# Hash attention with a SwiGLU layer: one pair's load moved between two groups of hash-bit DMAs, one head's hash moved by a slot

## The chip, the cores and the metric

The kernel runs on one core of one Trainium2 chip. The metric is device time in microseconds (us) of one execution; lower is better.

## The reference

Four batches, eight heads, 768 tokens, head width 64. Each query and key is hashed to six sign bits, and a query attends only to keys of the same bucket. The result goes through an RMS norm and a SwiGLU layer.

```python
q_bits = (einsum('bhsd,dk->bhsk', q, proj) > 0)      # proj: 64 x 6
k_bits = (einsum('bhsd,dk->bhsk', k, proj) > 0)
mask = q_bucket[:, :, :, None] == k_bucket[:, :, None, :]
scores = where(mask, q @ k.T / sqrt(64), -1e9)
attn = softmax(scores)                                # with 1e-9 in the sum
x = (attn @ v), heads side by side                    # 3072 x 512
xn = x / sqrt(mean(x * x) + 1e-6) * rms_g
out = (silu(xn @ w_gate) * (xn @ w_val)) @ w_out      # 512 -> 1536 -> 512
```

## The kernel before

**The work.** A unit `w` is half a batch of queries (384), so there are eight units, two to a batch. A *pair* (b, hp) is two neighbouring heads of batch b; (1, 3) is batch 1's last pair, heads 6 and 7. A *slot* is one step of 256 keys for one head and unit: `scores` (L338) makes two matmuls into PSUM, `probs` (L349) takes the exponential on ScalarE (ACT), and some slots later `av` (L357) multiplies with v. There are 192 slots. Slots 0 to 47 are batch 0's two units, in the order of `TURNS`; from slot 48 on units 2 to 7 follow, 24 slots each. Unit 2's pairs (1, 0), (1, 1), (1, 2), (1, 3) begin at slots 48, 54, 60 and 66.

**How masking works.** The tile `QK` holds a pair's k and q in fp16, 64 rows of data and twelve rows of hash bits below them. The bits are scaled so that unequal buckets push the score far down. So slot 48 can be computed only when rows of data *and* rows of bits of its pair are there.

**A pair's way.** The rows of k and q are loaded by SyncE (SP): `load_rows` (L107) as one DMA of 384 KB, or, for pairs (1, 2) and (1, 3) and all of batches 2 and 3, `load_blocks` (L115), four DMAs of 96 KB in short rows. Transposes on TensorE (PE) with a copy on VectorE (DVE) (`keep_pair`, L169 and L177), or, for the block-loaded pairs, on DVE alone (`turn_dve`, L193) give `T0`, the fp32 transposed form. Casts on GpSimd (POOL) and ACT bring it to `QK`. For the hash, small fp32 matmuls on PE (`hash_bank`, L209) fill a PSUM bank, and one DVE instruction (`signs`, L216) makes the bits. These then move to their twelve rows: as DVE copies and one SP DMA per head for heads 2 and 3 (`hash_head`, L247 and L249), or as eight SP DMAs per pair in batch 1 (`hash_pair`, L267, for pairs (1, 0) and (1, 1); `hash_lone`, L284, for (1, 2) and (1, 3)).

**Order.** It is written out by hand. `plan[s]` lists what is emitted at slot s, and `at(s, f, ...)` adds to it; ranks order the entries of a slot, equal ranks keep the order in which they were added. Each step of the last loop emits `scores(s + 1)`, the entries of rank below 3, `probs(s + 1)`, and then the rest. Each engine works its own instructions in that order, so one that waits holds those behind it. SP issues all loads of q, k and v, the bits DMAs and the stores; the weights are loaded by POOL (L520, L526). At most eight of SP's DMAs are under way at once: the ninth waits for the first of them to land, since they use eight semaphores in turn.

**Buffers.** The raw rows of q, k and v share ten buffers (`lpool`), taken in order of emission. Hash, transposes, gate, value and projection share three PSUM banks (`gps`). Scores have two PSUM buffers of their own.

**Around the change.** Head 2 of batch 0 is the first of pair (0, 1). Its k and q are transposed at slots 1 and 2, those of head 3 at slots 4 and 5. Its bits are needed from slot 12 on. Batch 1's pairs (1, 0) and (1, 1) are hashed at slots 32 and 41, each with eight bits DMAs on SP. The k, q and v of (1, 3) are loaded at slots 42, 44 and 47; its k is transposed by DVE at slots 52 to 55, its q at 56 to 59. From slot 48 on unit 0's SwiGLU layer runs between the scores: `gate` (L445, then a tanh on ACT, L447, and `a` on DVE, L457) and `value` (L455, L458).

Of the kernel before, what the change touches and what calls it, by code (L numbers as in the profile page):

```python
# [43 lines left out]
def kernel(  # L44
# [528 lines left out]
    def at(s, f, *a, rank=3):  # L573
        plan[s].append((rank, len(plan[s]), lambda: f(*a)))
# [23 lines left out]
            at(s + 1, casts, 0, hp, i)  # L598
        at(sv, v_prep, 0, hp)

    for h, s in ((2, 3), (3, 7)):
        at(s, hash_one, h)
        for t in range(3):
            at(s + 1 + t, lambda h=h, t=t: moves[h]((nc.vector,), t), rank=5)
# [26 lines left out]
    def in_row(loads, s, hash_slot=None):  # L631
        return loads, range(s, s + 8), (s + 4, s + 8, s + 9), hash_slot

    work = {
        (1, 2): ((21, 23, 30), (36, 37, 40, 40, 48, 49, 50, 51), (42, 52, 46), 53),
        (1, 3): in_row((42, 44, 47), 52, 61),
        (2, 0): in_row((51, 56, 59), 61), (2, 1): in_row((64, 67, 70), 71, 80),
        (2, 2): in_row((73, 76, 79), 81), (2, 3): in_row((82, 85, 88), 91, 100),
        (3, 0): in_row((94, 98, 102), 106), (3, 1): in_row((104, 108, 112), 116, 125),
# [118 lines left out]
```

## Time and profile before

| | |
|---|---|
| device time, median of 3 runs | 337.61 us (337.46 to 338.91) |
| profiled execution: its own time | 339.3 us |
| profiled execution: span, first to last instruction | 337.5 us |
| granted TensorE clock | 0.999 |
| PE, DVE, ACT, POOL busy | 326.8, 236.4, 210.0, 155.3 us |
| SP's DMA queue (q1), POOL's (q0) | 26.09 MB, 4.72 MB |

All times inside the execution are us from the span's start. A timeline line gives start, duration, engine, line, operation, output and inputs, count, and in brackets the idle time ahead of it with what ended it. Neighbouring instructions of one kind are merged ("x4"). "SPq" is SP's issuing of a DMA, not the transfer. In a table by stretches each engine has its busy time and, in brackets, its instructions, then come the granted clock, the mean busy share of the 16 DMA engines, and GB/s. In the list of waits the numbers are us in total, times, and the longest.

### The profile page before, as it was taken

The page shows a single profiled execution, that of the slowest core. Times are in us where ns is not written, and L with a number is a line of the kernel's source. Part 1 is how long each engine was busy: PE and PEld are TensorE (multiplying, and loading weights), DVE is VectorE, ACT ScalarE, POOL GpSimd, SP SyncE. Part 2 cuts the span into 40 slices and gives each one's busy share as a digit, 9 for nine tenths or more (in the row PEclk, how much of TensorE's full clock was granted, in tenths as well). Part 3 has the DMA queues.
Part 4 walks back from the last instruction along what each step waited for, and adds up shares of the span by engine and source line. Part 5 has one row for each costly group of instructions (what it writes and reads, how often), then busy time and mean ns, then how long its engine had stood idle before and what let it go on. Part 6 is the DMA issues. An engine that isn't in the chain of part 4 may idle for free.

```text
span 337.5 us, 7796 instructions
## 1 busy us (share of the span) xinstructions
PE 326.8 (97%) x2993; PEld 201.0 (60%) x2993; DVE 236.4 (70%) x526; ACT 210.0 (62%) x328; POOL 155.3 (46%) x230
## 2 busy tenths in 40 slices
PE   8999989889999999999999999999999999999995
PEld 7566656455566565566555666566556665655653
DVE  4769798688758896668768897557546663883860
ACT  3789987656666575757666676567667675332321
POOL 4878789836465576245736475613111311110000
PEclk9999999999999999999999999999999999999999
DMA  7999999464376064508243261100010001001002
GB/s 238 330 223 260 169 169 187 75 124 100 79 186 118 15 111 119 104 20 168 69 105 84 44 116 64 35 16 0 33 62 2 3 0 64 33 0 64 32 0 93
DMA packets 80244, 31.36 MB, mean 93 GB/s; under 512 B 65240, under 2 KB 77264, under 8 KB 80208
## 3 DMA queue, kind: packets, MB, share of 16 engines
q1 hardware_dynamic: 76272, 26.09, 31.7%
q0 software_dynamic: 3712, 4.72, 8.8%
q8 instruction: 23, 0.38, 0.5%
q14 instruction: 13, 0.11, 0.1%
q10 hardware_dynamic: 224, 0.07, 0.1%
HBM read 28.32 MB, written 6.29 MB: 103 GB/s over the span
## 4 chain that ended last, share of the span: by engine, by line
PE 85%; DVE 6%; SPq 3%; DMA 2%; ACT 2%; issue 1%; DVEq 0%; ACTq 0%
PE y_ps L469 18%; PE v_ps L455 17%; PE s_ps L343 15%; PE g_ps L445 12%; PE o_ps L365 9%; PE s_ps L445 5%; PE d_ps L209 4%; SPq L267 2%; PE t_ps L169 1%; PE x_ps L430 1%; PE z_ps L336 1%; DMA kL<-in_k_dram 1%; DVE otmp L380 1%; DVE xn L423 1%; ACT psb L353 1%
## 5 line engine op out<-in xcount | busy, mean ns | idle before, releaser
L353 ACT ACTIVATE psb<-s_ps 128x768 f16<-128x768 f32 x192 | 150.8, 808 | 28.1 <-PE s_ps L343 26.9
L343 PE MATMUL s_ps<-QK 76*128 76x384 f16 x384 | 93.5, 325 | 1.3 <-ACT psb L353 0.5
L455 PE MATMUL v_ps<-xnT,wv 128*128 128x384 f16 x384 | 78.1, 326 | 0.1
L469 PE MATMUL y_ps<-wo,ht 128*128 128x512 f16 x276 | 69.2, 379 | 0.3 <-ACT ysb L476 0.3
L389 POOL TENSOR_TENSOR x<-otmp,rcp 128x384 f32<-128x384 f32 x31 | 25.7, 830 | 93.0 <-DVE rcp L385 92.7
L365 PEld LDWEIGHTS <-psb 128*128 128x128 f16 x1152 | 51.6, 97 | 25.5 <-issue 7.5
L447 ACT ACTIVATE t<-g_ps 128x384 f32<-128x384 f32 x72 | 35.3, 490 | 43.6 <-PE g_ps L445 43.4
L458 DVE SCALAR_TENSOR_TENSOR ht<-a,v_ps 128x384 f16<-128x384 f32 x96 | 53.2, 554 | 10.7 <-PE v_ps L455 1.5
L457 DVE SCALAR_TENSOR_TENSOR a<-t,g_ps 128x384 f32<-128x384 f32 x72 | 39.5, 548 | 28.5 <-ACT t L447 28.3
L445 PE MATMUL g_ps<-xnT,wg 128*128 128x384 f16 x288 | 58.6, 325 | 0.7 <-DVE a L457 0.5
L365 PE MATMUL o_ps<-vl,psb 128*128 128x65 f16 x1152 | 56.8, 194 | 0.6 <-DVE otmp L380 0.5
L455 PEld LDWEIGHTS <-wv 128*128 128x128 f16 x384 | 36.4, 97 | 23.9 <-issue 0.5
L445 PEld LDWEIGHTS <-wg 128*128 128x128 f16 x384 | 36.0, 97 | 24.4 <-issue 1.1
L343 PEld LDWEIGHTS <-QK 76*128 76x128 f16 x384 | 31.6, 98 | 16.1 <-issue 3.7
L469 PEld LDWEIGHTS <-ht 128*128 128x128 f16 x276 | 25.9, 97 | 24.0 <-issue 0.6
L476 ACT COPY ysb<-y_ps 128x512 f32<-128x512 f32 x23 | 13.5, 585 | 25.5 <-PE y_ps L469 22.8
L431 DVE TENSOR_TENSOR xnT<-x_ps,gcol 128x512 f16<-128x512 f16 x24 | 16.3, 685 | 15.1 <-PE x_ps L430 15.1
L401 POOL TENSOR_TENSOR sq<-x 128x384 f32<-128x384 f32 x31 | 25.6, 826 | 2.4
L380 DVE TENSOR_TENSOR otmp<-o_ps,cvb 128x390 f32<-128x390 f32 x32 | 17.8, 558 | 8.8 <-PE o_ps L365 8.7
L447 ACT ACTIVATE t<-s_ps 128x384 f32<-128x384 f32 x24 | 11.8, 491 | 18.4 <-PE s_ps L445 17.6
L201 POOL CAST QK<-kT 64x768 f16<-64x768 f32 x20 | 16.8, 838 | 12.4 <-DVE kT L193 6.5
L193 DVE STREAM_TRANSPOSE kT<-kL 128x192 f32<-128x192 f32 x40 | 19.8, 517 | 2.7 <-DMA kL<-in_k_dram 2.7
(80 smaller groups left out, 325.7 us busy)
## 6 DMA issues: line engine op xcount, KB each, us to landing
vL<-in_v_dram SPq DMA_DIRECT2D x16, 384.0 KB
out_dram<-ysb SPq DMA_DIRECT2D x23, 256.0 KB
kL<-in_k_dram SPq DMA_DIRECT2D x40, 96.0 KB
qL<-in_q_dram SPq DMA_DIRECT2D x40, 96.0 KB
kL<-in_k_dram SPq DMA_DIRECT2D x5, 384.0 KB
qL<-in_q_dram SPq DMA_DIRECT2D x5, 384.0 KB
wg<-in_moe_w_gate_dram POOLq DMA_DIRECT2D x2, 768.0 KB, 7.2
wv<-in_moe_w_val_dram POOLq DMA_DIRECT2D x2, 768.0 KB, 8.5
```

The costliest lines, as they stand in the source:

```text
L343: nc.tensor.matmul(ps[:, j, 0:HALF], k_cols(w // 2, h, 2 * p + j), q_cols(w, h), start=True, stop=True,)
L353: nc.scalar.activation(psb[w, h][:, p], sps.pop(g)[:, :, 0:HALF], AF.Exp, scale=ESCALE,)
L365: nc.tensor.matmul(o[:, c, hh, 0:65], psb[w, h][:, jt // 2, jt % 2, 128 * c : 128 * c + 128], vls[b % 2][:, h, v_chunk(b, h, jt), 0:65], s ...
L380: nc.vector.tensor_add(tmp[:, :, :, 0:65], o[:, :, :, 0:65], cvb[b % 2][:, 2 * hp : 2 * hp + 2, 0:65].unsqueeze(1).to_broadcast([128, 3, 2 ...
L389: eng.tensor_mul(xd.rearrange("p c (h d) -> p c h d", h=2), tmp[:, :, :, 0:64], r.to_broadcast([128, 3, 2, 64]),)
L401: nc.gpsimd.tensor_mul(sq, xd, xd)
L445: nc.tensor.matmul(g, wg[:, kt, fs], xnT[w][:, kt], start=(kt == 0), stop=(kt == 3))
L447: nc.scalar.activation(t, g, AF.Tanh, scale=0.5)
L455: nc.tensor.matmul(vv, wv[:, kt, fs], xnT[w][:, kt], start=(kt == 0), stop=(kt == 3))
L457: nc.vector.scalar_tensor_tensor(out=a, in0=t, scalar=1.0, in1=g, op0=ALU.add, op1=ALU.mult)
L458: nc.vector.scalar_tensor_tensor(out=ht[w][:, ft], in0=a, scalar=0.5, in1=vv, op0=ALU.mult, op1=ALU.mult)
L469: nc.tensor.matmul(y, ht[w][:, ft, c * 128 : (c + 1) * 128], wo[:, ft, :], start=(ft == 0), stop=(ft == NF - 1),)
```

## The change

Two numbers of the written-out order. Head 2 of batch 0 is hashed at slot 4 instead of 3; its three DVE copies of bits, always one to three slots after it, move along. The k of pair (1, 3) is loaded at slot 38 instead of 42, and its q at 43 instead of 44; v stays at 47.

```diff
-    for h, s in ((2, 3), (3, 7)):
+    for h, s in ((2, 4), (3, 7)):
         at(s, hash_one, h)
         for t in range(3):
             at(s + 1 + t, lambda h=h, t=t: moves[h]((nc.vector,), t), rank=5)
...
     work = {
         (1, 2): ((21, 23, 30), (36, 37, 40, 40, 48, 49, 50, 51), (42, 52, 46), 53),
-        (1, 3): in_row((42, 44, 47), 52, 61),
+        (1, 3): in_row((38, 43, 47), 52, 61),
```

What it moves in each engine's order: on PE, head 2's four hash matmuls go behind the two matmuls of slot 5's scores and the three of head 3's k transpose. On DVE, head 2's signs go behind the copy of head 3's k, and one of its bit copies goes behind head 3's signs. On SP, the four DMAs of (1, 3)'s k go ahead of the eight bits DMAs of (1, 1); everything else keeps its place. ACT and POOL have the same order as before.

## The prediction

> **What bounds the kernel now.** I read the page first: TensorE (PE) is busy nearly all the time, at full granted clock.
>
> ```profile
> span 337.5 us, 7796 instructions
> PE 326.8 (97%) x2993; PEld 201.0 (60%) x2993; DVE 236.4 (70%) x526; ACT 210.0 (62%) x328; POOL 155.3 (46%) x230
> ```
>
> So only PE's 10.7 us of holes can be won. The table by stretches of 10 us says where: from 80 us to the end of the main loop PE is full, and the worst stretch is the one in which batch 1's last pair (1,3) is loaded.
>
> ```profile
> 60.00:70.00 10.00, 7.84 (x65) 4.23 (x64) 6.92 (x17) 4.84 (x9) 6.49 (x10) 1.00 0.63 111
> 70.00:80.00 10.00, 9.93 (x94) 6.10 (x94) 8.78 (x21) 6.61 (x11) 4.24 (x6) 1.00 0.42 72
> ```
>
> The timeline of PE, then of DVE, in that stretch shows the hole and its owner:
>
> ```profile
> 65.84 0.81 PE L455 MATMUL v_ps<-xnT,wv 128*128 128x384 f16 x4
> 68.30 0.29 PE L324 MATMUL m_ps<-vsum,ones 128*128 128x260 f16 x1 [1.65 <-DVE bits L216]
> 69.10 0.81 PE L445 MATMUL g_ps<-xnT,wg 128*128 128x384 f16 x4 [0.51 <-DVE a L457]
> 67.28 0.52 DVE L193 STREAM_TRANSPOSE kT<-kL 128x192 f32<-128x192 f32 x1 [2.73 <-DMA kL<-in_k_dram]
> 67.64 0.60 DVE L216 TENSOR_SCALAR bits<-d_ps,thr,scl 128x384 f16<-128x384 f32 x1
> ```
>
> DVE stands 2.73 us for the k rows of (1,3). Behind that transpose, in DVE's order, are the signs of (1,2)'s hash and the gate's `a`, which free PSUM banks; PE waits for both, 1.65 + 0.51 = 2.16 us. Why the rows are late is in SyncE's (SP's) timeline and the chain of waits:
>
> ```profile
> 34.62 6.73 SPq L121 DMA_DIRECT2D kL<-in_k_dram  x4
> 46.65 14.63 SPq L267 DMA_DIRECT2D QK<-bits  x16
> 61.39 3.06 SPq L121 DMA_DIRECT2D kL<-in_k_dram  x4
> 71.15 6.18 SPq L284 DMA_DIRECT2D QK<-bits  x8
> 63.86 3.29 DMA kL<-in_k_dram
> 72.83 1.79 DMA QK<-bits
> ```
>
> The sixteen bits DMAs of pairs (1,0) and (1,1) hold SP from 46.65 to 61.28, at 0.76 us each; the k rows come behind them and land at 67.15. SP has no rest from 54.42 to 80.83: it is issue after issue.
>
> The other place is batch 0's third head. Its hash stands ahead of slot 5's scores and waits for its own k and q copies:
>
> ```profile
> 11.94 0.49 PE L343 MATMUL s_ps<-QK 76*128 76x384 f16 x2
> 12.84 0.83 PE L209 MATMUL d_ps<-kT,pk 128*32 128x384 f32 x2 [0.41 <-DVE kT L177]
> 13.30 0.51 PE L209 MATMUL d_ps<-qT,pq 128*32 128x384 f32 x1
> ```
>
> **Part 1, the hash a slot later.** No instruction is added. On PE the four matmuls go behind slot 5's scores and the fourth head's k transpose; on DVE the signs go behind one more copy, and the three bit copies go to slots 5 to 7. SP's bits DMA for this head still waits for the signs, and the next SP wait, for the fourth head's signs (18.65), is unchanged in order. PE was held from 12.27 (slot 4's scores done) to 14.08: 1.81 us for a hash that takes 0.79 unhindered (17.05 to 17.84, head four). That is 1.02 us lost. In the new order slot 5's scores need the exponential of slot 3, which ends at 11.81 + 0.81 = 12.62, so 0.35 of it stays; then the transpose (0.33) ends at 13.32, when q's copy (12.70 + 0.55 = 13.25) is there, and the hash runs through. Gain up to 0.7 us at slot 9. The bits are needed at slot 12 (20.64) and their last copy comes at about 17.5, so I exclude a loss. Until slot 48 ACT is the tight engine (9.17 and 9.45 of 10 us in 20 to 40), and it follows PE. But what is not computed does not follow: scores of slot 48 sit at 54.55, right when (1,0)'s first bits land behind a queue of row loads. The weight loads ahead of those are issued by POOL in slot order, so I expect most of it to come through: 0.6 us, bounds 0 and 0.7.
>
> **Part 2, the k rows between the bits.** Four issues of about 0.68 us move ahead of (1,1)'s eight; q's slot change alters no order. The tile's buffer was last read by POOL's cast of v at 34.75 to 35.67, long before. SP is held at 52.1 by one more wait, the eighth bits DMA of (1,0), which takes the place of an outstanding v load (2.3 us, to 54.42). So the k issues run from 55.2 to about 58.2 and, with the 2.7 us from the last issue's end (64.45) to landing (67.15), the rows land near 61. DVE wants them at 64.55. The 2.73 us wait goes, and PE's 2.16 with it.
>
> Queued behind the moved load are (1,1)'s bits. The first two are needed by slot 54's scores (63.37). Their issues now start at about 58.3 and 59.1; landing 1.79 after the start as at 72.83, or behind the k rows at 61, they are there by 61.5: 1.9 us of slack, no cost.
>
> What is late next is SP itself. Slot 60's scores (75.78) need the first three bits DMAs of (1,2), which SP reaches at 71.15 after the same sum of issues in either order. The third landed at 74.62. PE without its stall would be at 73.6, so it meets a new wait. How long depends on SP's hesitations between 55.1 and 72.8. Unhindered, groups of four row issues take 2.70 (as at 88.04), v 0.59, bits 0.76 each, 0.1 between groups: 55.13 + 2.80 + 6.15 + 2.74 + 0.69 + 2.80 + 0.10 = 70.41 instead of 71.15, third landing 70.41 + 1.52 + 1.79 = 73.72. Then slot 60 gains up to 75.78 - 73.8 = 2.0. With the hesitations of before it gains 75.78 - 74.7 = 1.1. With 0.5 more, because the k issues now meet the tail of a weight load (share 1.23 of the DMA engines in 56 to 57), 0.6. The same queue serves (1,3)'s bits for slot 66, with about the same limits. So Part 2 gives 0.6 to 2.0; I take 1.3, between the same hesitations and none.
>
> **Sum.** The profiled execution took 339.3 us (span 337.5 and 1.8 around it). 339.3 - 0.6 - 1.3 = 337.4. The median shown is 337.61, 1.7 lower than that execution; the same 1.9 us off it gives 335.7.
>
> **Rivals.**
> *SP gives most of it back.* If SP is as hindered as now or more, and the early gain is swallowed by the bits' landing at 54.4, only 0.6 to 1.1 us remain: 336.5 to 337.0. For it: SP has not a microsecond of rest in 54 to 81. Against: its three long pauses there have no releaser that I can name.
>
> *Slower: the k issues are blocked by the weight load.* The same four issues for pair (1,2) took 6.73 us at 34.62 because the rows stood behind a weight load, against 2.70 when the DMA engines were free. Now they would start at 55.2, where the second half of the output weights is still moving (share above 1.2 until 57). If they take 6.73 again, SP is 3.6 us later for all that follows: slot 60's third bits DMA lands at 74.62 + 3.6 = 78.2 instead of the 75.78 at which PE came, 2.5 us late: 340.1. It turns slower once the four issues take over 3.06 + 1.1 = 4.2 us. Against: the share falls to 0.45 at 57 to 58, only 2 us in. [...]
>
> *No effect.* The hole at 66.65 goes but all of it comes back at slot 60, or slot 66: 337.6.
>
> **Chances.** A measurement of this kernel can tell about 0.5%, 1.7 us, from no change. Both parts as summed: 0.45, and its own range is 334.7 (0.7 and 2.16) to 335.9. Given back: 0.34. No effect: 0.08. Slower: 0.13. So faster by over 0.5% 0.45, within 0.42, slower 0.13. The range takes in the first three cases, 334.6 to 338.0, and leaves out the slower one.
>
> **What would show it.** Right: DVE's transposes of (1,3)'s k start without a DMA wait; the `m_ps` and `g_ps` waits of 1.65 and 0.51 are gone; SP issues four k rows between two groups of eight bits at about 55 to 58 in 3 to 3.6 us; at 12 to 14 us PE's hash shows no wait and slot 9 comes 0.7 earlier; a new PE wait for bits ahead of slot 60, under 1.5 us. Wrong: the k issues take over 4.2 us; PE waits for bits ahead of slot 54; PE's holes between 60 and 80 add up to as much as the 2.2 us of now; or slot 48 stands where it stood, so that Part 1 gave nothing.

## The result, and the profile after

The changed kernel takes 342.15 us (median of 6 runs, 340.28 to 343.13) where the kernel before took 337.53 beside it (6 runs, 336.52 to 343.11). The ratio is 1.0128 with a 95% interval of 1.0089 to 1.0168: slower. All ratios below are against the kernel before on the same chip; they leave out each kernel's executions that lie over 1.5% above its own fastest, so that a ratio can be smaller than the quotient of the medians (E2's above all).

The page of the changed kernel, in its head, shows the same busy time on PE and a span 1.0 us longer than the first profile of before:

```profile
span 338.5 us, 7796 instructions
PE 326.8 (97%) x2993; PEld 200.7 (59%) x2993; DVE 237.2 (70%) x526; ACT 210.0 (62%) x328; POOL 155.2 (46%) x230
```

The table by stretches of 10 us (PE's busy time is the second number) shows where. The hole of 60 to 70 is filled, 7.84 has become 9.83; but 70 to 80, which was full, now lacks 2.60:

```profile
60.00:70.00 10.00, 9.83 (x92) 5.71 (x89) 9.13 (x21) 6.21 (x10) 6.74 (x10) 1.00 0.33 55
70.00:80.00 10.00, 7.40 (x69) 4.57 (x67) 6.44 (x16) 5.36 (x9) 4.36 (x7) 1.00 0.40 84
```

PE's timeline names the owners. At 67.16 the gate waits 0.17 us where it waited 0.51 behind a hole of 1.65. At 76.60 slot 60's scores, the first of pair (1,2), wait 2.60 us in one piece for bits:

```profile
67.16 0.81 PE L445 MATMUL g_ps<-xnT,wg 128*128 128x384 f16 x4 [0.17 <-DVE a L457]
76.60 0.48 PE L343 MATMUL s_ps<-QK 76*128 76x384 f16 x2 [2.60 <-DMA QK<-bits]
```

SP's timeline, issue by issue, says why the bits are late. The k rows of (1,3) (53.84) stand between the two groups of eight bits as planned, but their four issues hold SP for 4.93 us; everything behind them slides, and (1,2)'s bits start at 72.82 instead of 71.15:

```profile
45.38 8.36 SPq L267 DMA_DIRECT2D QK<-bits  x8
53.84 4.93 SPq L121 DMA_DIRECT2D kL<-in_k_dram  x4
58.87 6.60 SPq L267 DMA_DIRECT2D QK<-bits  x8
65.58 2.71 SPq L121 DMA_DIRECT2D qL<-in_q_dram  x4
68.39 0.59 SPq L111 DMA_DIRECT2D vL<-in_v_dram  x1
69.08 3.63 SPq L121 DMA_DIRECT2D kL<-in_k_dram  x4
72.82 6.20 SPq L284 DMA_DIRECT2D QK<-bits  x8
```

In the list of waits this is one event, 2.6 us long, and it was not there before:

```profile
PE s_ps L343 <- DMA QK<-bits: 2.6, 1, 2.6
```

At the hash of batch 0's third head the PE timeline shows what the first edit did: the wait of 0.41 inside the hash is gone, slot 5's scores wait 0.24 for ACT instead, and at 22.73, ahead of slot 14, another wait for ACT has grown from 0.45 to 0.66:

```profile
13.15 0.49 PE L343 MATMUL s_ps<-QK 76*128 76x384 f16 x2 [0.24 <-ACT psb L353]
22.73 0.48 PE L343 MATMUL s_ps<-QK 76*128 76x384 f16 x2 [0.66 <-ACT psb L353]
```

One number of the result is in no line of this profile. The profiled execution had the full clock, span 338.5 and clock 1.000. The other five had clocks of 0.990 to 0.995 and spans of 339.2 to 341.4. Experiment A1 looks there.

**Theory and rivals after the result.** Theory: the load move costs, because the k issues are held by the output weights' transfer, SP reaches (1,2)'s bits late, and slot 60 waits; the long wait then also costs clock. Rivals: the hash move costs part of it; SP is late through the number of its issues, weights or not; the change has a price of its own besides SP's queue.

### The profile page after: what moved, and what is told of

The parts are those of the page before. It is cut to its first block, busy times and chain, and to the rows that moved or that the text cites. A ratio compares the mean times of both kernels' runs of the same rounds, so it can differ in the third digit from the quotient of the medians.

```text
span 338.5 us, 7796 instructions
## 1 busy us (share of the span) xinstructions
PE 326.8 (97%) x2993; PEld 200.7 (59%) x2993; DVE 237.2 (70%) x526; ACT 210.0 (62%) x328; POOL 155.2 (46%) x230
## 4 chain that ended last, share of the span: by engine, by line
PE 88%; DVE 5%; ACT 2%; DMA 2%; issue 1%; SPq 0%; POOL 0%; DVEq 0%; ACTq 0%
PE v_ps L455 18%; PE y_ps L469 17%; PE s_ps L343 16%; PE g_ps L445 14%; PE o_ps L365 10%; PE s_ps L445 5%; PE d_ps L209 4%; ACT psb L353 1%; PE t_ps L169 1%; PE x_ps L430 1%; DMA QK<-bits 1%; PE z_ps L336 1%; DVE otmp L380 1%; DVE xn L423 1%; DMA out_dram<-ysb 1%
## 5 line engine op out<-in xcount | busy, mean ns | idle before, releaser
L201 POOL CAST QK<-qT 64x768 f16<-64x768 f32 x20 | 16.7, 836 | 8.9 <-DVE qT L193 8.3
```

The costliest lines, as they stand in the source:

```text
L201: nc.gpsimd.tensor_copy(QK[b, hp][0:64, hh, o : o + S], T0[b, hp, which][64 * hh : 64 * hh + 64, :])
```

## The experiments

**E1 and E2, each part alone.** E1 is the kernel before with the hash edit, E2 the one with the load edit.

```diff
E1:
-    for h, s in ((2, 3), (3, 7)):
+    for h, s in ((2, 4), (3, 7)):
E2:
-        (1, 3): in_row((42, 44, 47), 52, 61),
+        (1, 3): in_row((38, 43, 47), 52, 61),
```

> The kernel before with the third head's hash at slot 4, loads untouched. Theory A (the changed kernel is slow because SP reaches the bits of pair (1,2) too late, after the moved k issues were blocked behind the output-weight load; the hash has little part in it): within 0.3% of the kernel before; DVE still stands 2 to 3 us for the k rows of (1,3), PE's holes of about 2.2 us at slot 56 stay. Theory B (the hash move costs, by delaying slots 5 to 48): over 0.8% slower than the kernel before. Theory C (the granted clock drops whatever the order, in both kernels): spans differ only with the clock listed.

> The kernel before with only the loads of (1,3) at slots 38 and 43. Theory A: as slow as the changed kernel, 1.0 to 1.5% over the kernel before; the four k issues take over 4 us, PE waits over 2 us for bits ahead of slot 60. Theory B: within 0.3% of the kernel before.

E1: 337.96 us against 338.29, ratio 1.0001 (0.9963 to 1.0040), so nothing that this interval can tell, in either direction. E2: 342.44 us against 338.29, ratio 1.0059 (1.0006 to 1.0111); ten of its twelve executions had a clock of 0.990 to 0.995, against nine of 29 of the kernel before beside it. The load move is what costs, though the ratio and the wait are less than expected (1.0 to 1.5%, over 2 us). E2's profile fell on one of the two executions with full clock; SP's timeline shows the k issues held for 5.67 us, and PE's a wait of only 0.81 ahead of slot 60. It is put down to POOL's `sq`, which the scores do not read. It ends 3.77 us behind SP's start at (1,2)'s bits, as the wait in the profile of after does (76.60 - 72.82 = 3.78), so it is the bits:

```profile
51.63 5.67 SPq L121 DMA_DIRECT2D kL<-in_k_dram  x4
70.58 6.20 SPq L284 DMA_DIRECT2D QK<-bits  x8
```

```profile
74.35 0.48 PE L343 MATMUL s_ps<-QK 76*128 76x384 f16 x2 [0.81 <-POOL sq L401]
```

**B1 and A1, both kernels profiled once more.** B1 is the kernel before, A1 the changed one, unedited.

> The kernel before, unchanged, profiled a second time. Its first profile took 337.5 us at clock 0.999; most executions of it list spans of 335.0 to 336.5 at clock 1.0. Theory A1 (DVE's wait for the k rows of (1,3) was an accident of the first profile): the wait is under 1 us here, PE's holes between 60 and 80 us are under 1 us, the span is 335 to 336. Rival: the wait of 2 to 3 us is there again and the span differs elsewhere.

> The changed kernel, unchanged, profiled a second time. Theory A with the clock: PE waits 2.5 to 4 us in one piece for bits ahead of slot 60 (or slot 48), and where the piece is long enough the granted clock falls to 0.5 for 3.4 to 6.4 us right behind it; span 339 to 341 at clock 0.995. Rival: the clock falls somewhere else, without a hole ahead of it.

B1 (336.74 us, span 334.9, clock 1.0) does not have the hole that the prediction was built on. Its SP timeline shows the sixteen bits in 12.36 us instead of 14.63, since the eighth of them was not held for a v load; the k rows are issued at 57.04 and are there in time. Its PE timeline has a wait of 0.16 where the first profile had 1.65 + 0.51:

```profile
44.57 12.36 SPq L267 DMA_DIRECT2D QK<-bits  x16
57.04 3.87 SPq L121 DMA_DIRECT2D kL<-in_k_dram  x4
67.54 6.35 SPq L284 DMA_DIRECT2D QK<-bits  x8
```

```profile
66.55 0.81 PE L445 MATMUL g_ps<-xnT,wg 128*128 128x384 f16 x4 [0.16 <-DVE a L457]
```

A1 (340.35 us, clock 0.994) waits as in the first profile of after, 2.65 us. Right behind the wait PE runs at half speed: a gate or value group of four matmuls takes 1.49 us instead of 0.81.

```profile
75.50 0.80 PE L343 MATMUL s_ps<-QK 76*128 76x384 f16 x2 [2.65 <-DMA QK<-bits]
76.09 1.49 PE L455 MATMUL v_ps<-xnT,wv 128*128 128x384 f16 x4
```

The table by stretches of 1 us (granted clock in the third column from the end) gives the size:

```profile
74.00:75.00 1.00, 0.00 (x0) 0.00 (x0) 0.68 (x2) 0.00 (x0) 0.00 (x0) 1.00 0.08 19
75.00:76.00 1.00, 0.50 (x2) 0.29 (x3) 0.00 (x0) 0.00 (x0) 0.00 (x0) 0.70 0.04 9
76.00:77.00 1.00, 1.00 (x4) 0.45 (x3) 0.00 (x0) 0.66 (x1) 0.00 (x0) 0.50 0.04 9
77.00:78.00 1.00, 1.00 (x12) 0.78 (x11) 0.38 (x1) 0.15 (x1) 0.00 (x0) 0.50 0.08 19
78.00:79.00 1.00, 1.00 (x7) 0.42 (x5) 0.60 (x3) 0.00 (x0) 0.22 (x2) 0.59 0.04 9
```

The clock that is missing is 0.30 + 0.50 + 0.50 + 0.41 = 1.71 us, that is 3.42 us at half speed. 1.71 of 340 is 0.0050: a clock of 0.995 over the whole span is one such drop, 0.990 is two.

**E3, (2,0)'s loads behind (1,2)'s bits.** The changed kernel; k, q and v of (2,0), and its transposes, three slots later, which takes four issues out of the queue ahead of slot 60.

```diff
-        (2, 0): in_row((51, 56, 59), 61),
+        (2, 0): in_row((54, 57, 60), 64),
```

> The changed kernel with the loads of pair (2,0) at slots 54, 57 and 60 instead of 51, 56 and 59 and its transposes three slots later, so that SP issues the eight bits DMAs of (1,2) before the four k DMAs of (2,0). Theory A: SP starts these bits 3 to 3.7 us earlier (about 69.2 instead of 72.8), PE has no wait ahead of slot 60, and the time falls by 2.5 us or more from the changed kernel, to the kernel before or up to 2 us below it. Theory B or C: no change from the changed kernel, over 0.8% slower than the kernel before.

340.36 us, ratio 1.0069 (1.0026 to 1.0113), not the full return that I expected. SP comes to (1,2)'s bits at 68.16 and slot 60 waits no more. But the k of (2,0) now stands with q and v ahead of (1,3)'s bits, and the wait moves to slot 66, with 1.49 us:

```profile
68.16 6.49 SPq L284 DMA_DIRECT2D QK<-bits  x8
74.75 2.70 SPq L121 DMA_DIRECT2D kL<-in_k_dram  x4
77.55 2.65 SPq L121 DMA_DIRECT2D qL<-in_q_dram  x4
81.00 6.62 SPq L284 DMA_DIRECT2D QK<-bits  x8
```

```profile
84.65 0.48 PE L343 MATMUL s_ps<-QK 76*128 76x384 f16 x2 [1.49 <-DMA QK<-bits]
```

**E4, the second half of the output weights later.** The changed kernel, with POOL's second `load_wo` at slot 52 instead of 39.

```diff
-        at(33 + 6 * i, load_wo, 6 * i, 6 * i + 6)
+        at(33 + 19 * i, load_wo, 6 * i, 6 * i + 6)
```

> The changed kernel with the second half of the output weights loaded at slot 52 instead of 39, so that no weight load runs beside the moved k issues. Theory A: the four k issues of (1,3) take 2.7 to 3.1 us instead of 4.93, SP starts the bits of (1,2) about 2 us earlier, PE's wait ahead of slot 60 falls from 2.6 to under 1 us, the time falls by 1.5 to 3 us from the changed kernel. If the block was not the weights: k issues still near 5 us, no change.

The time that I expected fell: 345.42 us, ratio 1.0198 (1.0152 to 1.0244). The mechanism is there, one step later. Without the weights beside them, (1,3)'s k issues take 2.70 us. The weights are issued at 65.51 instead, and now (2,0)'s k stands beside them, for 8.23 us; slot 60 waits 4.74:

```profile
53.55 2.70 SPq L121 DMA_DIRECT2D kL<-in_k_dram  x4
66.56 8.23 SPq L121 DMA_DIRECT2D kL<-in_k_dram  x4
74.89 6.20 SPq L284 DMA_DIRECT2D QK<-bits  x8
```

```profile
78.76 0.80 PE L343 MATMUL s_ps<-QK 76*128 76x384 f16 x2 [4.74 <-DMA QK<-bits]
```

**One law for slot 60.** Take the gate's matmuls at 66 to 67.2 (the lines with 0.15 to 0.17 above) as PE's own clock hand, and ask how much later SP starts (1,2)'s bits. In the first profile of after it is 72.82 - 67.16 = 5.66 with a wait of 2.60, so PE is in time up to 5.66 - 2.60 = 3.06. With this single constant these profiles come out (left out are E5 with its filler, E8, where PE lost time earlier, and the profiles with a hole of 0.5 or more at the mark itself):

| kernel | PE's mark | SP at (1,2)'s bits | lag | lag - 3.06 | wait measured |
|---|---|---|---|---|---|
| B1 (before) | 66.55 | 67.54 | 0.99 | none | none |
| E6 (below) | 66.82 | 67.73 | 0.91 | none | none |
| E3 | 66.72 | 68.16 | 1.44 | none | none |
| E2 | 66.70 | 70.58 | 3.88 | 0.82 | 0.81 |
| A1 (after) | 66.01 | 71.73 | 5.72 | 2.66 | 2.65 |
| E4 | 67.17 | 74.89 | 7.72 | 4.66 | 4.74 |

**E5, PE kept busy during the wait.** The changed kernel, with 36 idle 128x128 matmuls, whose result nobody reads, ahead of slot 60's scores.

```diff
-        idle(ps[:, 0, HALF:512], {0: 8, 3: 6}.get(g, 0))
+        idle(ps[:, 0, HALF:512], {0: 8, 3: 6, 60: 36}.get(g, 0))
```

> The changed kernel with 36 idle matmuls of 128x128 (about 2.0 us at 55 ns) on PE ahead of slot 60's scores; they write to an unused part of that slot's PSUM tile. They add no result. If long holes at slot 60 lower the clock: no drop behind slot 60, clock 0.998 or more in most executions, and since the filler lies within the hole the time falls by about 1.7 us from the changed kernel (1.0128), to 1.006 to 1.010 of the kernel before. If the drop has another cause: the clock stays at 0.995 and the time stays or grows by up to 2 us.

340.93 us, ratio 1.0070 (1.0033 to 1.0106) in place of 1.0128. Three of twelve executions had a clock under 0.998, where the changed kernel had five of six. The wait for bits itself is not shortened by this; so some 0.6% of the change's cost is clock that is lost behind the wait (the count of clocks says it more surely than the two ratios, whose intervals overlap). In its profile PE is busy throughout. How long it would have waited there without the filler is not shown: the lag of 70.73 - 66.84 = 3.89 alone would give 0.83, but the eight bits issues themselves take 7.48 us here instead of 6.20. Nor does the filler show as a cost: its executions with a clock of at least 0.998 have a median span of 338.7, after's one with full clock has 338.5.

```profile
70.00:80.00 10.00, 10.00 (x110) 6.71 (x106) 6.94 (x16) 5.81 (x10) 5.26 (x8) 1.00 0.29 48
```

**E6, only (2,0)'s k behind (1,2)'s bits, q and v behind (1,3)'s.** The changed kernel, with one number triple:

```diff
-        (2, 0): in_row((51, 56, 59), 61),
+        (2, 0): in_row((54, 62, 63), 69),
```

> The changed kernel with the loads of pair (2,0) at slots 54, 62 and 63 and its transposes from slot 69 on, so that SP issues the bits of (1,2) ahead of (2,0)'s k, and the bits of (1,3) ahead of its q and v. Theory A (SP's queue ahead of slots 60 and 66 is what costs): no PE wait for bits ahead of slot 60 and slot 66; the time falls 2 us or more from the changed kernel, to 0.997 to 1.003 of the kernel before, and what is left of clock drops comes from slot 48. If waits of other kinds are behind it: over 1.006, as the kernel with only (2,0)'s k moved.

338.49 us against 338.99, ratio 0.9999 (0.9963 to 1.0035); ten of twelve executions with a clock of at least 0.998. The k issues of (1,3) are still held by the weights, 6.06 us, but SP has four issues less ahead of slot 60 and reaches both sets of bits in time:

```profile
51.35 6.06 SPq L121 DMA_DIRECT2D kL<-in_k_dram  x4
67.73 6.21 SPq L284 DMA_DIRECT2D QK<-bits  x8
79.35 6.27 SPq L284 DMA_DIRECT2D QK<-bits  x8
```

With SP's queue shortened ahead of slots 60 and 66, then, nothing of the change's cost is left, to within 0.4%. It gains nothing either: DVE now has the transposes of (2,0) and (2,1) in the same slots, and PE waits for the gate behind them:

```profile
102.80 0.81 PE L455 MATMUL v_ps<-xnT,wv 128*128 128x384 f16 x4 [0.84 <-DVE a L457]
```

**E7, E6's edit on the kernel before.** The same triple, without the change.

> The kernel before (rows of (1,3) behind both groups of bits, third hash where it was), with the loads of pair (2,0) at slots 54, 62 and 63 and its transposes from 69 on: the same two queue positions as in the run with k alone ahead of (1,3)'s bits, but without the change. My theory: what the change costs is SP's queue ahead of slots 60 and 66. With that queue made shorter, before and after should be equal: against the kernel before this one comes out at 0.997 to 1.002, within 0.3% of the same edit on the changed kernel (0.9999), and slot 60 waits under 0.5 us for bits. Rival: the change costs something of its own that the freed queue only paid for; then this kernel is faster than the kernel before by 0.6 to 1.2% (335 to 336.5 where before takes 338.5), and the change's loss of 1% shows again between the two.

340.00 us against 337.37, ratio 1.0041 (1.0006 to 1.0075), with no clock under 0.999 in twelve executions. The rival (0.6 to 1.2% faster) is out; my own figures, 0.997 to 1.002 and within 0.3% of E6, were missed too, by 0.2% and 0.1%. Its PE timeline shows the original hole in a middle size, 1.28 us, where E6 has 0.17, and it pays for DVE's crowded slots as E6 does:

```profile
67.78 0.29 PE L324 MATMUL m_ps<-vsum,ones 128*128 128x260 f16 x1 [0.77 <-DVE bits L216]
68.58 0.81 PE L445 MATMUL g_ps<-xnT,wg 128*128 128x384 f16 x4 [0.51 <-DVE a L457]
```

With SP's queue lightened, then, the change looks like a gain of some 0.4% (1.0041 to 0.9999), as the prediction had it; the two intervals overlap, so this is not shown. Neither version beats the kernel before.

**E8, both halves of the output weights six slots earlier.** The changed kernel:

```diff
-        at(33 + 6 * i, load_wo, 6 * i, 6 * i + 6)
+        at(27 + 6 * i, load_wo, 6 * i, 6 * i + 6)
```

> The changed kernel with the two halves of the output weights loaded six slots earlier (27 and 33 in place of 33 and 39), so that the second has left the DMA engines when (1,3)'s k rows are issued. My theory: the four k issues take under 4 us (2.7 unhindered), SP comes to (1,2)'s bits by 70 to 71.5 in place of 73.3, slot 60's wait falls from 2.6 to under 1 us, fewer executions lose clock, and the ratio against the kernel before falls from 1.013 to 1.000 to 1.005; unless the weights block earlier rows instead, in which case DVE or PE wait 2 us or more for rows or bits between 40 and 57, and the ratio stays at 1.01. Rival, that SP is late through the number of its issues alone: slot 60 waits over 2 us although the k issues are short, and the ratio stays at 1.010 to 1.016.

The "unless" of the expectation came: 342.86 us, ratio 1.0156 (1.0103 to 1.0210). The k issues of (1,3) take 2.70 us, and slot 60 waits only 0.21 (put down to ACT, but again 3.77 behind SP's start at the bits, 73.98). But the weights now meet the rows of (1,2). The four issues of its q take 7.34 (2.66 in E7, with the weights where they were), and DVE stands 4.03 us for its k, issued before. Behind that PE loses 3.29 us before 49.78, with half the clock behind it (SP's timeline, DVE's, PE's, and a stretch of 2 us):

```profile
40.88 7.34 SPq L121 DMA_DIRECT2D qL<-in_q_dram  x4
57.88 2.70 SPq L121 DMA_DIRECT2D kL<-in_k_dram  x4
```

```profile
48.02 0.52 DVE L193 STREAM_TRANSPOSE kT<-kL 128x192 f32<-128x192 f32 x1 [4.03 <-DMA kL<-in_k_dram]
49.78 0.66 PE L365 MATMUL o_ps<-vl,psb 128*128 128x65 f16 x9 [3.29 <-DVE otmp L380]
```

```profile
52.00:54.00 2.00, 2.00 (x11) 0.48 (x9) 1.26 (x5) 1.22 (x2) 1.37 (x3) 0.50 1.13 219
```

The queue rival is not tested by slot 60 here, since PE came late itself; against it stand the issues, 2.70 without the weights in E4 and E8 and 4.38 to 6.06 with them in after, A1, E2, E5 and E6.

## Why the prediction was wrong

**The base.** The first step that failed is the one in which PE's 2.16 us were taken off the profiled execution, and the rest carried to the median by "the same 1.9 us off". The hole is not a property of the kernel but of that execution: four profiles with (1,3)'s k at its old place have 2.16 (the first), 0.16 (B1), 1.12 (E1: 0.61 + 0.51) and 1.28 (E7). The slower span of the profiled execution (337.5, where the executions of before with a clock of at least 0.998 have medians of 335.7, 336.3 and 335.35 in the three later comparisons) held part of that hole already. So the same time was counted twice, once as gain and once as distance to the median. The four profiles, two of them with other edits, average 1.2 us; about that much there was to win, before any new wait.

**SP's queue.** The sum 55.13 to 70.41 for (1,2)'s bits is the term that was mis-sized. The prediction allowed 15.28 us from the k issues' start to there. It measured 53.84 to 72.82, 18.98 us. With 0.1 between the groups: k of (1,3) 5.03 against 2.80, bits 6.71 against 6.15, q 2.81 against 2.74, v 0.69 as planned, k of (2,0) 3.74 against 2.80; 2.23 + 0.56 + 0.07 + 0.94 - 0.10 = 3.70. The largest is the k issues behind the weights, for which the prediction had put "0.5 more". The argument against it, that the share of the DMA engines falls at 57 to 58, was read off the trace of before, where the rows were not yet in the queue. With them in it, the k issues end at 57.3 to 58.8 in after, A1, E2, E3 and E6 although they start anywhere from 51.35 to 54.66 (E3, the last to start, takes only 3.17). I read from this that the end of the weights' transfer lets them go, and not their own length: in after the second half of the weights lands at 58.8 (issued at 48.0, 10.8 us to landing), and the k issues end at 58.77. Why the k of (2,0) takes 0.94 more than planned, with no weights under way, is not shown.

**The rival that came.** "The k issues are blocked by the weight load", with its price of 2.5 us at slot 60 and its turning point of 4.2 us, had the mechanism: 4.93 us, a wait of 2.60, and in the execution with full clock 340.28 us against the 340.1 forecast. That the sizes agree so well is partly luck: the rival had the bits 3.6 us later than before and PE there at 75.78; they came 1.67 later, and PE was there at 74.00. It got 0.13 although a row spoke for it (6.73 us at 34.62, beside a weight load); against it stood only the author's estimate, from the trace of before, that the weights would be out of the way 2 us on. Four such issues take 2.70 us without the weights (E4, E8) and 4.38 to 8.23 beside them, in seven profiles (after, A1, E2, E4, E5, E6, E8). By what the weights hold them, no run here shows.

**What no case had.** Behind the wait the clock can halve (A1: 0.50 for 3.42 us). The full-clock execution of after has a span of 338.5, 2.8 over before's 335.7; the other five average 340.4, that is 1.9 more, about one drop of 1.71. Together that is about the 4.6 us between the medians.

**Part 1.** Step by step it did what was said (the wait in the hash is gone), but the term of 0.6 was too large. From slot 4's scores to slot 9's PE takes 5.64 us instead of 6.18, so 0.54 is gained. The longer wait for ACT takes back about half by slot 14 (10.31 instead of 10.57). The rest stays: to slot 47 it is 41.07 to 41.10 in after, A1 and E1 and 41.30 to 41.34 in before, B1 and E2. A gain of 0.24 us is far inside E1's interval of 0.4% to either side, so E1's 1.0001 neither shows nor denies it. The prediction named ACT as the tight engine of 20 to 40 by its 9.17 and 9.45 of 10 us; in the same two stretches PE has 9.46 and 9.46, so those rows did not single ACT out.

**Of the list of what would show it:** DVE's waits and the `m_ps` wait are gone, as said; "the k issues take over 4.2 us" and "PE's holes between 60 and 80 add up to as much" (0.17 + 2.60 against 2.2) both came on the wrong side.

## What to carry to other kernels

Before a hole is costed, see it in a second profile of the same kernel: one that owes its length to when a DMA landed can be 0.16 us in one execution and 2.16 in the next, and the median hardly holds it. A queue that issues without rest has no free place: moving an issue forward is paid by what stands behind it (here (1,2)'s bits came 1.67 us later), and beside a bulk transfer the issues can last about as long as that transfer (here the k issues ended at 57.3 to 58.8 in five profiles, wherever they started; E4 and E8 only moved the collision). Price idle time of PE in one piece at more than its length where a profile shows the clock drop behind it: here a wait of 2.65 us was followed by 3.42 us at a granted clock of 0.50 (A1).

## What the runs showed of the hardware

The granted clock falls to one half behind single waits of PE of 2.65 us (A1), 4.74 (E4), 3.29 (E8) and 2.35 (E1, whose profile caught a wait for bits ahead of slot 48), though not behind the 2.60 of after's first profile. It comes back after 3.42 us in A1 and, by the same sum, in E4 (0.13 + 0.50 + 1.00 + 0.08 = 1.71 us of clock missing from 78 to 83), and after twice that in E1 and E8 (3.41 us of clock missing in each). The mean clocks of after are 1.000, 0.994 to 0.995, or 0.990, that is none, one or two such pieces of 1.71 us. The kernel before loses it too, in 18 of the 68 executions beside the experiments (clocks of 0.988 to 0.995).

The length of the wait alone does not decide. In the 3.41 us ahead of the fall PE was idle for 1.92 us in E1, 2.55 in A1, 2.64 in E8 and all of it in E4; after has 2.60 us in one piece and no fall. An estimate of where the wait fell in after: E1's two pieces at half clock last 6.82 us together, 3.41 each, and the trace's record of full clock lasts 331.09 us in before (5.68 to 336.77) and in after (7.05 to 338.15) alike, which is 97 times 3.413. If the clock changes only at such steps, one of them, 77 ahead of 338.15, is at 75.32, inside the wait of after, with 1.32 and 1.28 us of idle time on its two sides (PE's busy time is the second number; two stretches of after, then the 3.42 us ahead of the fall in A1 and the 3.41 us ahead of it in E1):

```profile
71.91:75.32 3.41, 2.09 (x21) 1.15 (x18) 3.27 (x10) 2.38 (x4) 1.78 (x3) 1.00 0.53 82
75.32:78.73 3.41, 2.13 (x21) 1.43 (x22) 1.45 (x5) 0.81 (x1) 0.00 (x0) 1.00 0.05 11
71.98:75.40 3.42, 0.87 (x12) 0.35 (x8) 2.59 (x7) 1.39 (x3) 1.35 (x2) 1.00 0.24 40
52.28:55.69 3.41, 1.49 (x20) 1.00 (x18) 2.48 (x5) 1.74 (x3) 3.11 (x5) 1.00 1.20 243
```

Counted in the same way, the most idle time without a fall behind it is 1.69 us in before (67.12 to 70.53) and these 1.32 in after; their last stretches, behind which the clock does fall, have 2.73 and 3.15. Once at half, the clock stayed there for a second piece where PE was idle for 0.55 us (E1) or 0.65 us (E8) of the first, and came back after one piece with 0.10 us (A1) or under 0.03 (E4). So single waits of much the same length were followed by no piece at half clock (after, 2.60 us), one (A1, 2.65) or two (E1, 2.35).
